# One transfer for the mask, the third tile's side loads in wider transfers on GpSimd's queue, and eight transfer places counted by the list scheduler

## The chip, the cores and the metric

The kernel runs on one core of a Trainium2 chip. The metric is the device time of one execution in microseconds (us). Several executions are timed, and one more is recorded by the hardware profiler; its times say where the work lies. The engines are TensorE (PE; its weight loads are PEld), VectorE (DVE), ScalarE (ACT), GpSimd (POOL) and SyncE (SP), which only issues transfers. SP and ACT issue transfers here; the transfers themselves run on 16 DMA engines.

## The reference

Attention over 4 batches, 8 heads, 576 positions of 64 numbers. The first four heads see a band of 32 positions, the other four see every 32nd position up to their own. The result, 2304 tokens of 512 numbers, goes through two MLPs of 512 to 2048 to 512.

```python
scores = scale * np.matmul(q, k.transpose(0, 1, 3, 2))
mask_local = (rel >= 0) & (rel < stride)
mask_strided = (rel >= 0) & (pos[None, :] % stride == pos[:, None] % stride)
scores = np.where(masks, scores, -1e9)
attn = softmax(scores)
x = np.matmul(attn, v)                    # -> (2304, 512)
r = np.maximum(x @ w_in, 0.0)             # first MLP
x = (s * (r * r) + b) @ w_out
h = x @ w_in2                             # second MLP
g = np.where(h >= 1, h, np.where(h <= -1, 0.0, (h + 1) ** 2 / 4))
out = g @ w_out2
```

## The kernel before

**Attention tiles.** The attention is cut into 21 tiles, sorted by their first token: 12 "strided" ones, three for each batch (d = 0, 1, 2), and 9 "local" ones of 256 tokens. Tiles 0, 1 and 2 are the strided ones of batch 0, tiles 3, 4 and 5 are local ones, tile 6 is the first strided one of batch 1, and so on. `attend` (from L427) writes down one tile: its loads (L446 to L459, all through the helper `load`), two TensorE matmuls that put the mask into two PSUM banks (L562), the scores on top of it (L567 strided, L582 local), the softmax on DVE and ACT (L589 to L600), four transposes (L609, called flips here), a copy of them to `pt`, and the values' matmuls (L623 strided, L633 local) into two banks named `side`. The `side` banks are a pair; from tile 6 on the scores use the same pair. They are drained by ACT, which rounds to fp32r (`xh`), and by DVE, which takes the remainder (`xl`, L665). `xh` and `xl` are the input of the first MLP.

**The third tile.** The third strided tile of a batch (d = 2) gathers what the first two leave over: its keys `k3` and queries `q3` are loaded in part (L490 to L498, columns 18 to 90) and for the rest copied out of the first two tiles' keys and queries (GpSimd or ACT, L312). Its value rows come from five places of the input in runs of 18 and 54 rows (L509 to L516). For batch 0 these loads go through ACT's queue, for the other batches through SP's.

**The mask.** `masks` (L406) loads the mask of the strided tiles into `mask_t`, 54 rows of 54 twice, at partitions 0 and 64, and a tile `fix_t` with the local mask, the identity and two scalars. GpSimd fills `mask_t` with a large negative number before. The casts `bias_t` and `idb_t` to bf16 follow; the first scores need both.

**The MLPs.** The first MLP works on six units of 384 tokens. Each of its products is made of three matmuls, high by high, low by high and high by low (L682 to L684). A hidden block is four such triples into one bank `h`. Its weights are loaded as 64-bit numbers (`raw`, 512 KB, three buffers) and decoded: a step on ACT (L328), two on DVE (L330, L332), a rounded copy on ACT (`w0h`, `w1h`) and a remainder on DVE (`w0l`, `w1l`, L351). A `raw` buffer is free again when L332 has read it. The second MLP multiplies by a scheme with seven products for eight; its weights are prepared during the first one (L357 to L398), written to memory as `dw` and read back later.

**What sets the order.** The program writes down operations with their engines, planned durations and dependences. `Issue.order` then works out due times backwards from the end, subtracts each operation's `sooner`, adds a normal draw of size JITTER (0.3, SEED 3, one number for each operation in turn), and places the operations one at a time: the one that can start first, and among equals the one that is due first. The order of starts becomes the order of instructions on every engine and queue. `attend_upto` (L1000) sets `sooner` for all operations of a tile to AHEAD * max(at - 5, 0), which is 0 for the first tiles, and so overwrites what `masks` had set. A transfer is planned with its queue's time and a latency; how many are under way at once isn't planned. The first loads of SP and ACT go out at once, and later ones wait in their queue for a place.

## Time and profile before

| what | us |
|---|---|
| timed executions | 847.67, 849.72, 850.36 |
| median | 849.72 |
| profiled execution | 847.82 |
| its span | 846.0 |
| TensorE busy in the span | 824.3 (97%) |
| VectorE busy | 599.4 (71%) |
| ScalarE busy | 517.4 (61%) |
| GpSimd busy | 22.8 (3%) |

All rows below come from the profiled execution, whose time is its span and 1.8 us around it. A stretch a:b is the time from a to b us after the span's start. Idle time in brackets behind an instruction is the time that its engine stood before it, with what ended the wait. The clock granted to TensorE is given as a share of its upper level.

### The profile page before, as it was taken

How to read it: one execution, taken by the hardware profiler on the slowest of the kernel's cores; microseconds unless marked ns; L12 is line 12 of the kernel's file. 1: busy time of each engine (PE TensorE's matmuls, PEld its weight loads, DVE VectorE, ACT ScalarE, POOL GpSimd, SP SyncE). 2: the span in 40 equal slices, each digit the busy share in tenths (PEclk: the TensorE clock that was granted, in tenths of full speed). 3: DMA queues.
4: the chain of work that ended last, by engine and by line, in shares of the span. 5: the costliest groups of instructions: out<-in, count | busy, mean ns of one | idle time of the engine just before them, and what ended most of it. 6: DMA issues, size and time to landing. Idle time of an engine off the chain costs nothing.

```text
span 846.0 us, 17391 instructions
## 1 busy us (share of the span) xinstructions
PE 824.3 (97%) x6336; PEld 800.7 (95%) x6336; DVE 599.4 (71%) x1250; ACT 517.4 (61%) x1054; POOL 22.8 (3%) x62
## 2 busy tenths in 40 slices
PE   6789999999999999999999999999999999999998
PEld 3579998989999899999999999999999999999998
DVE  5788647475598785767678356897666998465966
ACT  3577645554577674556567467875477854577653
POOL 1110000010000000000001000000000000000000
PEclk9599999999999999999999999999999999999999
DMA  8858271363389994768785558888988788878883
GB/s 260 259 177 276 99 240 64 91 183 108 122 289 329 277 310 132 223 222 255 257 303 196 154 185 253 252 255 271 293 267 256 252 254 286 289 252 252 251 271 103
DMA packets 115930, 191.77 MB, mean 227 GB/s; under 512 B 13830, under 2 KB 57990, under 8 KB 115846
## 3 DMA queue, kind: packets, MB, share of 16 engines
q1 hardware_dynamic: 114818, 190.23, 70.7%
q8 instruction: 51, 0.84, 0.4%
q10 hardware_dynamic: 1028, 0.43, 0.2%
q14 instruction: 33, 0.27, 0.1%
HBM read 150.25 MB, written 40.37 MB: 225 GB/s over the span
## 4 chain that ended last, share of the span: by engine, by line
PE 84%; DMA 8%; DVE 4%; ACT 2%; issue 1%; SPq 1%; ACTq 0%; DVEq 0%
PE h L682 7%; PE acc L682 6%; PE acc L684 6%; PE acc L683 6%; PE h L683 6%; PE h L684 6%; PE acc L934 6%; PE acc L932 6%; PE acc L933 6%; PE side L934 5%; PE side L933 5%; PE side L932 5%; DMA raw<-in_w_ins 4%; PE h L934 3%; PE h L932 3%; PE h L933 3%
## 5 line engine op out<-in xcount | busy, mean ns | idle before, releaser
L704 ACT ACTIVATE t<-h 128x384 f32<-128x384 f32 x96 | 46.5, 485 | 62.6 <-PE h L684 62.2
L682 PE MATMUL acc<-gh,w1hx 128*128 128x384 f32 x192 | 65.2, 340 | 0.0
L682 PE MATMUL h<-xh,w0hx 128*128 128x384 f32 x192 | 65.1, 339 | 0.0
L683 PE MATMUL acc<-gl,w1hx 128*128 128x384 f32 x192 | 64.9, 338 | 0.2
L683 PE MATMUL h<-xl,w0hx 128*128 128x384 f32 x192 | 64.5, 336 | 0.0
L684 PE MATMUL acc<-gh,w1lx 128*128 128x384 f32 x192 | 64.5, 336 | 0.0
L684 PE MATMUL h<-xh,w0lx 128*128 128x384 f32 x192 | 64.2, 334 | 0.0
L310 ACT ACTIVATE gh<-t 128x384 fp32r<-128x384 f32 x96 | 50.0, 521 | 21.9 <-DVE t L717 21.3
L721 DVE TENSOR_TENSOR gl<-t,gh 128x384 fp32r<-128x384 f32 x92 | 51.0, 555 | 16.1 <-ACT gh L310 15.8
L717 DVE TENSOR_SCALAR t<-t,fix_t 128x384 f32<-128x384 f32 x77 | 36.7, 477 | 35.8 <-ACT t L708 35.5
L682 PE MATMUL acc<-gh,w1h 128*128 128x384 f32 x168 | 57.2, 340 | 0.0
L684 PE MATMUL acc<-gh,w1l 128*128 128x384 f32 x168 | 56.9, 339 | 0.0
L683 PE MATMUL acc<-gl,w1h 128*128 128x384 f32 x168 | 56.8, 338 | 0.0
L682 PE MATMUL h<-xh,w0h 128*128 128x384 f32 x144 | 50.8, 353 | 0.2 <-ACT t L704 0.2
L683 PE MATMUL h<-xl,w0h 128*128 128x384 f32 x144 | 49.4, 343 | 0.0
L684 PE MATMUL h<-xh,w0l 128*128 128x384 f32 x144 | 49.3, 342 | 0.0
L708 ACT ACTIVATE t<-t 128x384 f32<-128x384 f32 x79 | 41.4, 524 | 2.1
L683 PEld LDWEIGHTS acc<-gl,w1hx 128*128 128x128 f32 x192 | 36.0, 188 | 1.1 <-DVE gl L721 1.0
L682 PEld LDWEIGHTS acc<-gh,w1hx 128*128 128x128 f32 x192 | 36.0, 188 | 0.4
L682 PEld LDWEIGHTS h<-xh,w0hx 128*128 128x128 f32 x192 | 36.0, 188 | 0.3
L683 PEld LDWEIGHTS h<-xl,w0hx 128*128 128x128 f32 x192 | 36.1, 188 | 0.0
L684 PEld LDWEIGHTS h<-xh,w0lx 128*128 128x128 f32 x192 | 36.1, 188 | 0.0
(513 smaller groups left out, 2514.3 us busy)
## 6 DMA issues: line engine op xcount, KB each, us to landing
w0h<-dw SPq DMA_DIRECT2D x84, 256.0 KB
w0l<-dw SPq DMA_DIRECT2D x84, 256.0 KB
w0hx<-dw SPq DMA_DIRECT2D x84, 256.0 KB
w0lx<-dw SPq DMA_DIRECT2D x84, 256.0 KB
raw<-in_w_ins SPq DMA_DIRECT2D x32, 512.0 KB
raw<-in_w_outs SPq DMA_DIRECT2D x32, 512.0 KB
dw<-pt SPq DMA_DIRECT2D x48, 256.0 KB
dw<-po SPq DMA_DIRECT2D x48, 256.0 KB
```

The source lines that it names most:

```text
L310: e.activation(out=out, in_=in_, func=AF.Copy)
L682: e.matmul(out=acc, lhsT=wh, rhs=ah, start=first, stop=False)
L683: e.matmul(out=acc, lhsT=wh, rhs=al, start=False, stop=False)
L684: e.matmul(out=acc, lhsT=wl, rhs=ah, start=False, stop=last)
L704: op(lambda e: e.activation(out=c(t), in_=c(p), func=AF.Relu), [act(n)], [p], [t])
L708: e.activation(out=c(t), in_=c(t), func=AF.Square)
L717: e.tensor_scalar(out=c(t), in0=c(t), scalar1=sb_t[:, 0:1], scalar2=sb_t[:, 1:2], op0=MUL, op1=ADD)
L721: op(lambda e: e.tensor_tensor(out=c(gl), in0=c(t), in1=c(gh).bitcast(F32), op=SUB), [pool(n)] + [dve2(n)], [t, gh], [gl])
L932: e.matmul(out=dst, lhsT=wh, rhs=ah, start=opens and first, stop=False, skip_group_check=not opens)
L933: e.matmul(out=dst, lhsT=wh, rhs=al, start=False, stop=False, skip_group_check=not opens)
L934: e.matmul(out=dst, lhsT=wl, rhs=ah, start=False, stop=last, skip_group_check=not opens)
```

## The change

1. **Mask.** `fix_t` is loaded first, and the mask in one transfer of 128 rows: its source runs twice over 64 rows of the input (step 0, then 64 rows). The rows 54 to 63 of each half come from the input too.
2. **Third tile's keys and values.** The keys are loaded by head pair, two transfers of 128 partitions, whose source is two blocks of 64 rows, in place of two of 64 partitions. The values are loaded in three transfers (36, 54 and 54 rows) in place of six (18, 18, 54, 18, 18, 18), written as one operation in place of three.
3. **Queue.** For batch 0 these six transfers are issued by GpSimd, planned at 1.0 us each, and no longer by ACT. For the other batches they stay on SP.
4. **Places.** The scheduler keeps a list of eight places (`LANES`). A transfer that is not GpSimd's starts in the plan only when places are free, and holds them until its planned end.
5. **`sooner`.** `attend_upto` adds to what stands there, so what `masks` sets now counts.

Lines after L72 stand one to six lines lower than before; L447, L324, L312 and L665 of before are L453, L330, L318 and L671 after.

```diff
@@ -69,6 +69,7 @@
 DMA_RATE = 390.0e3
 DMA_LATENCY = 2.0
 DMA_ISSUE = 0.45
+LANES = 8
 
 
 class Buf:
@@ -86,7 +87,7 @@
 
 
 class Op:
-    __slots__ = ("fn", "engs", "deps", "succ", "allocs", "bufs", "due", "wait", "ready", "start", "eng", "n", "behind", "sooner", "idle")
+    __slots__ = ("fn", "engs", "deps", "succ", "allocs", "bufs", "due", "wait", "ready", "start", "eng", "n", "behind", "sooner", "idle", "dmas")
 
 
 class Issue:
@@ -98,8 +99,9 @@
     def __init__(self):
         self.ops, self.apart = [], []
 
-    def op(self, fn, engs, reads=(), writes=(), part=(), after=(), allocs=(), line=None):
+    def op(self, fn, engs, reads=(), writes=(), part=(), after=(), allocs=(), line=None, dmas=0):
         o = Op()
+        o.dmas = dmas or any(x[0] == "sp" for x in engs)
         o.fn, o.engs, o.n, o.succ, o.due = fn, engs, len(self.ops), [], None
         deps = set(after)
         o.behind, o.sooner = (), 0.0
@@ -158,7 +160,7 @@
         rng = np.random.default_rng(SEED)
         for o in self.ops:
             o.due += JITTER * rng.standard_normal() - o.sooner
-        free = {"port": 0.0}
+        free, lanes = {"port": 0.0}, [0.0] * LANES
         for o in self.ops:
             o.wait, o.ready = len(o.deps), 0.0
             for x in o.engs:
@@ -187,6 +189,8 @@
                     continue
                 for e, d, _, *port in o.engs:
                     at = max(free[e], o.ready, t, free["port"] if port else 0.0)
+                    if o.dmas and e != "pool":
+                        at = max(at, lanes[o.dmas - 1] - DMA_ISSUE * (o.dmas - 1))
                     key = (at + (d - min(x[1] for x in o.engs)), o.due, o.n, d, at)
                     if best is None or key < best[0]:
                         best = (key, o, e, d)
@@ -200,6 +204,8 @@
             if port:
                 free["port"] = at + d
             end = at + d + lag
+            if o.dmas and e != "pool":
+                lanes = sorted(lanes[o.dmas:] + [end] * o.dmas)
             for b in o.allocs:
                 b.ring.taken.append(b)
             for b in o.bufs:
@@ -404,9 +410,9 @@
         return b * S if kind == "s" else t * 256
 
     def masks():
-        op(lambda e: e.dma_start(out=fix_t, in_=fixed[:, 128 + KT:FW]), [("act", 0.5, DMA_LATENCY)], writes=[fix_buf]).sooner = 50.0
-        op(lambda e: [e.dma_start(out=mask_t[g * 64:g * 64 + 54, 0:54], in_=fixed[0:54, 0:54]) for g in range(2)],
-           [("act", 1.0, DMA_LATENCY)], part=[mask_buf[0]]).sooner = 49.0
+        op(lambda e: e.dma_start(out=fix_t, in_=fixed[:, 128 + KT:FW]), [("act", 0.5, DMA_LATENCY)], writes=[fix_buf], dmas=1).sooner = 80.0
+        op(lambda e: e.dma_start(out=mask_t[:, 0:54], in_=bass.AP(fixed.tensor, fixed.offset, [[0, 2], [FW, 64], [1, 54]])),
+           [("act", 0.5, DMA_LATENCY)], part=[mask_buf[0]], dmas=1).sooner = 49.0
         op(lambda e: copy(e, bias_t[:, 0], mask_t), [("dve", 0.15, 0.1)], [mask_buf[0]], [bias_buf[0]]).sooner = 50.0
         op(lambda e: copy(e, idb_t, id_t), [("dve", 0.2, 0.1)], [fix_buf], [idb_buf]).sooner = 50.0
 
@@ -442,9 +448,9 @@
             return buf(wp if tag[0] == "w" else sp, tag, [128, 512], F32, BUFS.get(tag, MS // 2))
 
         def load(y, parts, size, queue="sp", line=a_line):
-            ways = [dma(size, len(parts)) if queue == "sp" else ("act", DMA_ISSUE * len(parts), DMA_LATENCY + 2 * size / DMA_RATE)]
+            ways = [dma(size, len(parts)) if queue == "sp" else (queue, 1.0 * len(parts), DMA_LATENCY + 2 * size / DMA_RATE)]
             first = bool(w_loads) and not held and line is a_line
-            o = op(lambda e, i=i: [e.dma_start(out=f(), in_=x) for f, x in parts], ways, part=[y], line=line,
+            o = op(lambda e, i=i: [e.dma_start(out=f(), in_=x) for f, x in parts], ways, part=[y], line=line, dmas=len(parts),
                    after=[w_loads[k] for k in HOLD] if first else ())
             if first:
                 held.append(o)
@@ -456,7 +462,8 @@
             return o
 
         half = lambda par: slice(par * D, (par + 1) * D)
-        side = ("act", b_line) if b == 0 else ()
+        side = ("pool", b_line) if b == 0 else ()
+        view = lambda x, at, *dims: bass.AP(x.tensor, x.offset + at, [list(n) for n in dims])
         W = RT * NJ
         QC, VC = 4 * 128, 4 * 128 + 2 * W
         if strided and d < 2:
@@ -491,9 +498,9 @@
                 rest[b] = [buf(sp, f"{n}3", [128, 2, 144], F32) for n in "kq"]
                 k3, q3 = rest[b]
                 src = strd[b, 4]
-                rest[b] += [load(k3, [(lambda par=par: k3.tile[half(par), :, 18:90],
-                                       src[half(par), 0:512].rearrange("p (h a n) -> p h a n", h=2, a=2)[:, :, par, 0:72])
-                                      for par in range(2)], 128 * 144 * 4, *side),
+                rest[b] += [load(k3, [(lambda h=h: k3.tile[:, h, 18:90],
+                                       view(src, 256 * h, (64 * SW + 128, 2), (SW, 64), (1, 72))) for h in range(2)],
+                                 128 * 144 * 4, *side),
                             load(q3, [(lambda: q3.tile[:, :, 18:90], src[:, QC:VC].rearrange("p (h n) -> p h n", h=2)[:, :, 0:72])],
                                  128 * 144 * 4, *side)]
             k3, q3, k_load, q_load = rest[b]
@@ -509,11 +516,10 @@
             ins, vals = [kb_, qb_], [vb_]
             v4 = lambda: vb_.tile.rearrange("p (g n) -> p g n", g=2)
             src = strd[b, 4]
-            parts = [(lambda: v4()[0:18, 0], strd[b, 3][108:126, VC:SW]), (lambda: v4()[18:36, 0], src[0:18, VC:SW]),
-                     (lambda: v4()[0:54, 1], src[18:72, VC:SW])]
-            parts += [(lambda t=t: v4()[64 + 18 * t:82 + 18 * t, 0], strd[b, t][108:126, VC:SW]) for t in range(3)]
-            for j in range(3):
-                load(vb_, parts[2 * j:2 * j + 2], 48 * 1024, *side)
+            parts = [(lambda: v4()[0:36, 0], view(strd[b, 3], 108 * SW + VC, (20 * SW, 2), (SW, 18), (1, 4 * D))),
+                     (lambda: v4()[0:54, 1], src[18:72, VC:SW]),
+                     (lambda: v4()[64:118, 0], view(strd[b, 0], 108 * SW + VC, (128 * SW, 3), (SW, 18), (1, 4 * D)))]
+            load(vb_, parts, 160 * 1024, *side)
             groups2 = [(j, g, n, (lambda par, hp, c=c, n=n: kb_.tile[half(par), hp, c:c + n]),
                         (lambda par, hp, c=c, n=n: qb_.tile[half(par), hp, c:c + n]), at_)
                        for j, g, n, c, at_ in ((0, 0, 36, 0, 0), (1, 0, 54, 90, 0), (0, 1, 54, 36, 36))]
@@ -1004,7 +1010,7 @@
             attend(at, first_token(at) < U0[1])
             at += 1
             for o in plan.ops[begin:]:
-                o.sooner = AHEAD * max(at - 5, 0)
+                o.sooner += AHEAD * max(at - 5, 0)
 
     pend = []
     todo = [(0, i) for i in range(KP)] + [(1, i) for i in range(KP)]
```

**What moves at the start.** ACT's queue from its first instruction on, before (`k_3` and `q_4` are the third tile's keys and queries, `w1hx` its values, `xh_2` holds tile 0's keys and queries, `sm` the scores before the exponential):

```order
L408 DMA mask_t<-in_fixed 54x54 x2
L407 DMA fix_t<-in_fixed 128x226
L447 DMA k_3_145<-in_strd 64x2x72 x2
L447 DMA q_4_151<-in_strd 128x2x72
L447 DMA w1hx_153<-in_strd 18x256 x2
L310 ACTIVATE bias_t<-fix_t 32x64 x4
L447 DMA w1hx_153<-in_strd 54x256
L447 DMA w1hx_153<-in_strd 18x256
L310 ACTIVATE k_3_145<-xh_2_131 64x2x18 x2
L447 DMA w1hx_153<-in_strd 18x256 x2
L595 ACTIVATE sm_166<-sm_166 128x512
```

The same of after:

```order
L413 DMA fix_t<-in_fixed 128x226
L414 DMA mask_t<-in_fixed 128x1x54
L316 ACTIVATE bias_t<-fix_t 32x64 x4
L316 ACTIVATE k_3_132<-xh_2_130 64x2x18 x4
L316 ACTIVATE q_4_147<-xh_2_130 128x2x18 x2
L601 ACTIVATE sm_166<-sm_166 128x512
```

Two transfers are left, and four copies that GpSimd had (two of `k_3`, two of `q_4`) stand behind the casts. GpSimd's queue after, from its last memset on; `xl_15` holds tile 1's keys and queries:

```order
L1063 MEMSET bias_t 32x32 x4
L453 DMA k_3_132<-in_strd 128x1x72 x2
L453 DMA q_4_147<-in_strd 128x2x72
L453 DMA w1hx_157<-in_strd 36x1x256
L453 DMA w1hx_157<-in_strd 54x256
L453 DMA w1hx_157<-in_strd 54x1x256
L318 COPY q_4_147<-xl_15_162 128x2x18
L318 COPY k_3_132<-xl_15_162 64x2x18 x2
```

Six transfers stand ahead of the copies from `xl_15`.

**What moves on VectorE ahead of the first hidden block.** Before (`side_650` and `side_651` are the banks of tile 4's values, `dt_686` the decode of the third weight):

```order
L330 TENSOR_SCALAR dt_686<-dt_686 128x512
L665 TENSOR_TENSOR xl_136<-side_651,xh_135 128x2x2x32
L665 TENSOR_TENSOR xl_134<-side_651,xh_133 128x2x2x32
L332 SCALAR_TENSOR_TENSOR dt_686<-raw_573,dt_686 128x512
L665 TENSOR_TENSOR xl_136<-side_650,xh_135 128x2x2x32
L665 TENSOR_TENSOR xl_134<-side_650,xh_133 128x2x2x32
L351 TENSOR_TENSOR w0l_563<-dt_618,w0h_562 128x512
```

After (there the banks are `side_648` and `side_649`, and the third weight is `dt_637`):

```order
L336 TENSOR_SCALAR dt_637<-dt_637 128x512
L338 SCALAR_TENSOR_TENSOR dt_629<-raw_556,dt_629 128x512
L338 SCALAR_TENSOR_TENSOR dt_637<-raw_570,dt_637 128x512
L671 TENSOR_TENSOR xl_138<-side_648,xh_137 128x2x2x32
L671 TENSOR_TENSOR xl_136<-side_648,xh_135 128x2x2x32
L671 TENSOR_TENSOR xl_138<-side_649,xh_137 128x2x2x32
L671 TENSOR_TENSOR xl_136<-side_649,xh_135 128x2x2x32
```

The last step of that decode, a SCALAR_TENSOR_TENSOR, stood between the drains of the two banks; now both drains follow behind it. On TensorE the scores of tile 6 and the first hidden block now stand ahead of the values of tile 5, which came first before.

**What moves on SP behind the loads of tile 7.** Before (`xl_140` is tile 7's keys and queries, `qx_775` its values, `qv_831` the values of tile 8, `raw` weights):

```order
L447 DMA xl_140_747<-in_strd 128x2x764
L447 DMA qx_775<-in_strd 54x2x256 x2
L324 DMA raw_805<-in_w_ins 128x512
L447 DMA qv_831<-in_strd 18x256 x2
L447 DMA qv_831<-in_strd 54x256
L447 DMA qv_831<-in_strd 18x256 x3
L324 DMA raw_886<-in_w_outs 128x512
L324 DMA raw_907<-in_w_outs 128x512
```

After:

```order
L453 DMA xl_140_703<-in_strd 128x2x764
L330 DMA raw_749<-in_w_ins 128x512
L330 DMA raw_773<-in_w_outs 128x512
L330 DMA raw_821<-in_w_outs 128x512
L453 DMA qx_841<-in_strd 54x2x256 x2
L453 DMA qv_884<-in_strd 36x1x256
L453 DMA qv_884<-in_strd 54x256
L453 DMA qv_884<-in_strd 54x1x256
```

Three weights stand ahead of tile 7's values now, where one stood behind them. From there to 230 us the order on the engines differs in many places by a few rows; the decodes come one or two hidden blocks sooner. From about 235 us on TensorE's order is the same in both.

## Rows read from the trace of the kernel before

**Rows 1.** The page, parts 1 and 3: busy us of each engine, then the transfer queues.

```profile
PE 824.3 (97%) x6336; PEld 800.7 (95%) x6336; DVE 599.4 (71%) x1250; ACT 517.4 (61%) x1054; POOL 22.8 (3%) x62
...
q1 hardware_dynamic: 114818, 190.23, 70.7%
...
q10 hardware_dynamic: 1028, 0.43, 0.2%
```

**Rows 2.** Busy time by stretches: stretch, its length, engines (instructions), PE clock, DMA share, GB/s.

```profile
8.00:12.00 4.00, 4.00 (x96) 2.69 (x84) 2.33 (x6) 1.88 (x7) 0.68 (x4) 0.57 0.78 229
12.00:30.00 18.00, 12.73 (x354) 8.93 (x352) 15.42 (x47) 7.15 (x20) 3.20 (x7) 0.87 1.03 305
...
39.00:46.00 7.00, 6.63 (x82) 5.84 (x84) 4.23 (x10) 3.46 (x9) 0.87 (x3) 0.52 0.68 218
46.00:54.00 8.00, 8.00 (x104) 7.24 (x105) 6.78 (x16) 6.14 (x14) 1.29 (x2) 1.00 0.57 192
54.00:66.00 12.00, 8.58 (x143) 6.70 (x142) 11.71 (x29) 9.71 (x26) 1.82 (x2) 1.00 0.50 165
66.00:70.00 4.00, 4.00 (x16) 3.99 (x15) 3.86 (x10) 2.31 (x5) 0.00 (x0) 0.57 1.02 380
...
290.00:320.00 30.00, 27.57 (x152) 25.99 (x151) 24.92 (x51) 22.93 (x48) 0.00 (x0) 1.00 0.86 274
```

**Rows 3.** Timeline of 0:12, all engines: start, us, engine, line, operation, idle before and releaser.

```profile
1.19 0.91 ACTq L408 DMA_DIRECT2D mask_t<-in_fixed  x2
...
2.13 0.37 ACTq L407 DMA_DIRECT2D fix_t<-in_fixed  x1
...
2.54 3.04 ACTq L447 DMA_DIRECT2D k<-in_strd  x2
...
6.33 0.20 DVE L312 CAST bias_t<-mask_t 128x64 bf16<-128x64 f32 x1 [5.20 <-DMA mask_t<-in_fixed]
...
7.44 0.39 PE L562 MATMUL acc<-bias_t,idb_t 128*128 128x256 bf16 x2 [2.18 <-DVE idb_t L312]
...
9.25 0.21 POOL L312 COPY q<-xl 128x36 f32<-128x36 f32 x1 [3.39 <-DMA xl<-in_strd]
...
10.43 0.63 ACT L595 ACTIVATE sm<-sm 128x512 f32<-128x512 f32 x1 [0.41 <-issue]
...
11.28 0.87 PE L567 MATMUL acc<-k,q 64*36 64x36 f32 x24
```

**Rows 4.** Timeline of 12:30, TensorE.

```profile
20.88 0.46 PE L582 MATMUL acc<-xl 64*32 64x64 f32 x32 [1.40 <-DMA xl<-in_loc]
...
28.35 0.30 PE L633 MATMUL side<-pt,w1lx 64*64 64x32 f32 x4 [1.35 <-DMA qv<-in_loc]
```

**Rows 5.** Timeline of 33:42, TensorE and VectorE.

```profile
38.48 0.68 DVE L332 SCALAR_TENSOR_TENSOR dt<-raw,dt 128x512 int32<-128x512 int32 x1
...
38.82 0.42 PE L633 MATMUL side<-pt,qx 64*64 64x32 f32 x4 [1.29 <-DVE xl L665]
39.08 0.48 DVE L665 TENSOR_TENSOR xl<-side,xh 128x128 fp32r<-128x128 f32 x2
...
39.48 1.28 DVE L351 TENSOR_TENSOR w0l<-dt,w0h 128x512 fp32r<-128x512 f32 x2
...
39.62 0.96 PE L633 MATMUL side<-pt,qx 64*64 64x32 f32 x26 [0.37 <-DVE xl L665]
```

**Rows 6.** Timeline of 30:46, SP's queue.

```profile
35.32 0.47 SPq L447 DMA_DIRECT2D xl<-in_strd  x1
40.72 1.14 SPq L447 DMA_DIRECT2D qx<-in_strd  x2
41.97 0.36 SPq L324 DMA_DIRECT2D raw<-in_w_ins  x1
```

**Rows 7.** Timeline of 54:66, VectorE and TensorE.

```profile
56.08 0.75 DVE L593 TENSOR_TENSOR sx<-side,mx 128x256 f32<-128x256 f32 x2
...
56.75 0.80 PE L623 MATMUL side<-pt,qv 54*64 54x54 f32 x32 [1.27 <-ACT gh L310]
```

## The prediction

> **What bounds the kernel now.** I read the busy shares first, then the stretches, then inside the bad stretches the timeline with its waits. TensorE works for 824.3 of 846.0 us [rows 1], so 21.7 us of idle TensorE is all that any change of order or of transfers can win, beside stretches at the lower clock. Stretch less busy time gives where they lie [rows 2]: 5.27 us in 12:30, 0.37 in 39:46, 3.42 in 54:66, and late in the kernel 2.43 in 290:320. The clock ran near its lower level in 8:12, 39:46 and 66:70 (granted 0.57, 0.52, 0.57; 1.00 is the level of 2.4 GHz), the last two of them behind stretches in which TensorE stood and waited.
>
> Three things hold TensorE there. At the start it is the transfers: the DMA engines are full from 2 us on but sag to 0.78 in 8:12 [rows 2], and the scores of local tiles wait 1.40 us at 20.88 for a load, the values of tile 3 another 1.35 at 28.35 [rows 4]. From 38 us it is VectorE's place in the chain of the first hidden block [rows 5]. In 54:66 it is VectorE outright: 11.71 of 12 us busy [rows 2], while TensorE waits for banks it has to drain [rows 7]. (The profile names ACT's gh as the releaser at 56.75; the values' matmul there needs no gh, it needs the banks that VectorE was reading at 56.08.)
>
> **The change, part by part.** The sum is made on the profiled execution, 847.82 us = span 846.0 + 1.82. The median of the runs, 849.72, lies 1.90 above it, and I carry the difference over to the median.
>
> *Start-up.* Before, ACT issues the mask (0.91), the fixed tile (0.37), the third tile's keys (3.04, most of it waiting) and the rest [rows 3]; the exponential of the first tile starts at 10.43 after 0.41 of idle that its input doesn't explain: ACT still issues. After, ACT issues two transfers and GpSimd the other six. The fixed tile's issue moves from 2.13 to about 1.19, 0.94 sooner; TensorE has stood 2.18 us when the cast of its identity lets it start at 7.44, and the mask's cast was done at 6.53, so 0.9 is open here if the mask stays in time. The DMA engines' sag in 8:12 is worth 4 x (1 - 0.78) = 0.88 us of transfer; with six issues gone from the shared places, SP's loads wait less, and that is what TensorE waits for at 20.88 and 28.35. These are one chain, not a sum: I take -0.9, from 0 to -1.4 (0.9 + the exponential's 0.41). ACT takes over four small copies from GpSimd, about 0.2 each like GpSimd's at 9.25; the 7 us up to the exponential cover them, and without that cover they would cost 0.8.
>
> *GpSimd's queue.* The trace shows no transfer issued by GpSimd. The nearest rows are ACT's issues: 0.37 for one transfer, up to 3.04 for two with waiting [rows 3]; six of them take 2.2 to 9.1 us. Behind them on GpSimd stand the copies that fetch tile 1's part of the third tile's keys, at 9.25 before. From about 1.7, behind its first memsets, the issues end at 3.9 to 10.8, so 0 to +1.6; I take 0, since an issue that waits for no place is what the lower row shows.
>
> *Mask and keys in wider pieces.* Mask: one issue fewer, 0.46, counted above. How a transfer spreads is seen in the queue's count: q10 carries 1028 packets [rows 1], of which 892 are rows of data (108 mask, 128 fixed tile, 256 keys, 256 queries, 144 values). The other 136 come out exactly as 9 per transfer of 54 or 18 rows and 16 per transfer of 64 or 128 rows, one per DMA engine that took part. So a row count is dealt to 16 engines or to its largest divisor below. What a source in two blocks of 64 (mask, keys) does, no row shows: 16 engines by its 128 rows, or 2 by its outer count. I take 16 for the sum and give the other its own rival. The Trainium skill, "DMA: Bandwidth & Descriptors", section "Why a DMA increments its semaphore by 16 and not by 1", says that the slowest dimension of both patterns decides, which would make it 2 here; with that rule the start-up term would be lost and not -0.9. Its rule for single dimensions agrees with the 9 and 16 of this count.
>
> *Order of the first hidden block.* The draw of numbers shifts, since eight operations fall away, so lines move where no transfer did. Before, VectorE does the last step of the third weight's decode, 0.68, between the drains of the two banks, for which TensorE waits 1.29 at 38.82 and 0.37 at 39.62 [rows 5]; after, it stands ahead of both. The second drain then ends some 0.6 sooner, so the 0.37 goes and the 1.29 for the first stays. What comes behind is the scores of tile 6 in place of the values of tile 5, work that is done either way. -0.4; 0 if the decode's data are late, -1.66 if both waits go.
>
> *Weights ahead of the values on SP.* SP stands 4.9 us behind xl until the buffer of qx is free at 40.72; the first weight behind it goes out at 41.97 [rows 6]. After, three weights stand ahead of qx. The first then waits only for its own buffer, free before the third weight's step ends at 39.16 [rows 5]: at least 2.8 us sooner. One weight costs VectorE 0.68 for that step and 1.28 / 2 = 0.64 for the remainder, 1.32 us with its short first step left out [rows 5]. In 39:54 VectorE has 15 - 4.23 - 6.78 = 3.99 us free, in 54:66 0.29 [rows 2]. Each weight decoded in the first frees 1.32 in the second, where TensorE stood 3.42. The pairs of banks there are also drained behind more matmuls than before. I take -1.4, one weight's worth. Bounds: all of the 3.42 and the slow clock behind it, 66:70 at 0.57 costs 4 x (1 - 0.57) = 1.72, so -5.1; on the other side +1.4, one weight decoded in the wrong place. qx itself goes out later by what the three weights wait, and the loads of the third tile's values behind it with it; both are first used in 54:66 or after, some 15 us on, and cost nothing.
>
> *Later batches.* Three issues fewer each on SP, hidden by loads that run ahead: 0. The order of loads also changes between 231 and 318 us, where weights come from memory; TensorE's order there stays. 0, from -2.43 (all idle of 290:320) to +3.8 (two loads of 512 KB put ahead at that stretch's 274 GB/s, 1.9 each) [rows 2].
>
> Sum: -0.9 - 0.4 - 1.4 = -2.7. That gives 845.1 on the profiled execution and **847.0** on the median.
>
> **Rivals.** (A) The forecast, -2.7: 847.0, with its own range 845.0 to 849.0.
>
> (B) *The count of places does not do what it says.* It is a number in the planner; the first fourteen loads of SP stand in the same order as before. If the sag in 8:12 has another cause, and VectorE, 15.42 of 18 us busy in 12:30 [rows 2], sets the pace anyhow, only the -0.4 is left: 849.3. Against it: ACT's issue of keys, 3.04 for two, shows a queue that waits.
>
> (C) *Slower: few engines take the mask and the keys.* By the row count above, 2 engines get 64 packets each. A packet of SP's queue takes 0.707 x 16 x 846 / 114818 = 83 ns, one of q10 0.002 x 16 x 846 / 1028 = 26 ns [rows 1]. Alone, 64 take 1.7 us; taking turns with SP's, 64 x 109 ns = 7.0. The mask took 6.33 - 2.10 = 4.2 us from its issue's end [rows 3], with 12 packets to an engine; it would land between 7.6 and 12.9 and the first scores start up to 5.6 late. The keys' two transfers, behind each other on the same engines, land as late as 20.6, where the third tile's scores stood at 11.28, 9.3 late. The waits at 20.88 and 28.35 absorb 1.40 + 1.35 = 2.75, and the later terms' -1.8 stays: 9.3 - 2.75 - 1.8 = +4.75, 854.5. It is slower from a lateness of 4.55 on. For it: the page's rule. Against it: packets can run in bursts, which is then B's result, and GpSimd's queue may spread otherwise.
>
> (D) *The whole VectorE gap closes*: -0.9 - 0.4 - 5.1 = -6.4, 843.3.
>
> **How the numbers follow.** 0.3%, 2.55 us, is about what a measurement of this kernel can tell. A 0.46 (of which 0.26 under 847.2, 0.20 within), B 0.24 (0.20 within, 0.02 to either side), C 0.20 (0.18 slower, 0.02 within), D 0.10. Faster 0.26 + 0.02 + 0.10 = 0.38; same 0.20 + 0.20 + 0.02 = 0.42; slower 0.02 + 0.18 = 0.20. The range takes in D's value and C up to a lateness of 7.8 us: 843.0 to 853.0. A alone is 845.0 to 849.0.
>
> **What would show it.** Start-up right: the first scores before 7.0, the exponential right behind its input, the wait at 20.88 under 0.6, DMA over 0.9 in 8:12. C: mask's cast after 8 us, or the third tile's scores waiting for keys. First block right: its first matmul before 40.5, with nothing of a decode between the drains. Weights right: VectorE busier in 39:54, TensorE over 10 of 12 us in 54:66, and the clock at its upper level in 66:70. Wrong would be: the same TensorE idle before 70 us, or a new wait for a weight in 290:320.

## The result and the profile after

The changed kernel is slower. Its median is 855.32 us against 849.73 us of the kernel before, both over five executions; the ratio is 1.0067, 95% interval 1.0047 to 1.0088. Measured again beside the experiments (g1_changed below), it is 855.81 against 847.75, ratio 1.0086 (1.0053 to 1.0118). The forecast was 847.0 with a range of 843.0 to 853.0; the time lies outside it, on the other side of the time before.

The profiled execution took 857.9 us, with a span of 855.4 against 846.0 before. It is the longest of the five, and the one of before is near its shortest: the profiles lie 10.1 us apart, the medians 5.6. The page, engines and transfer queues:

```profile
PE 824.1 (96%) x6332; PEld 800.8 (94%) x6335; DVE 601.3 (70%) x1258; ACT 514.5 (60%) x1048; POOL 27.7 (3%) x66
...
q1 hardware_dynamic: 114614, 190.23, 70.4%
...
q0 software_dynamic: 464, 0.30, 0.2%
...
q10 hardware_dynamic: 274, 0.14, 0.1%
```

TensorE works 824.1 us, as before [rows 1]. What came in this profile is idle time, 855.4 - 824.1 = 31.3 us against 21.7. The stretches, in the same columns as [rows 2]:

```profile
2.00:8.00 6.00, 3.17 (x9) 1.08 (x8) 0.23 (x1) 2.40 (x12) 4.02 (x6) 1.00 0.99 267
8.00:12.00 4.00, 0.00 (x0) 0.00 (x0) 0.00 (x0) 0.00 (x0) 0.00 (x0) 0.50 1.06 259
12.00:30.00 18.00, 12.52 (x336) 8.79 (x339) 13.00 (x37) 5.93 (x17) 1.55 (x7) 0.83 0.94 264
...
46.00:54.00 8.00, 8.00 (x125) 7.33 (x124) 5.55 (x14) 4.87 (x11) 1.05 (x6) 0.82 0.72 250
54.00:66.00 12.00, 10.50 (x147) 8.83 (x136) 11.78 (x28) 9.86 (x24) 3.60 (x5) 1.00 0.62 191
66.00:70.00 4.00, 3.71 (x83) 3.02 (x81) 4.00 (x11) 2.90 (x6) 0.52 (x1) 1.00 0.76 240
70.00:230.00 160.00, 153.91 (x1804) 145.02 (x1806) 95.91 (x238) 80.71 (x172) 7.84 (x22) 0.97 0.42 132
...
290.00:320.00 30.00, 27.70 (x155) 26.43 (x154) 27.11 (x55) 23.47 (x48) 0.00 (x0) 1.00 0.95 306
```

Two places carry the new idle time. In 8:12 no engine but the DMA engines does anything: 4.00 us of idle, where TensorE was busy throughout before. And in 70:230, 160 - 153.91 = 6.09 us are idle. Before, that stretch had 0.04, and 66:80 nothing:

```profile
66.00:80.00 14.00, 14.00 (x74) 13.99 (x73) 10.73 (x24) 10.59 (x21) 0.00 (x0) 0.88 0.86 289
70.00:230.00 160.00, 159.96 (x1941) 151.19 (x1940) 99.28 (x240) 87.09 (x183) 7.01 (x22) 1.00 0.44 137
```

On the other side 54:66 gained what the forecast had hoped for, 1.50 us of idle against 3.42, and 290:320 stayed.

The first place, in the timeline:

```profile
1.60 1.85 POOL L453 DMA_DIRECT2D k<-in_strd  x2
1.63 1.12 ACTq L414 DMA_DIRECT2D mask_t<-in_fixed  x1
...
2.44 0.47 SPq L453 DMA_DIRECT2D xl<-in_strd  x1
2.96 1.22 SPq L453 DMA_DIRECT2D w0lx<-in_strd  x2
3.42 0.77 POOL L453 DMA_DIRECT2D q<-in_strd  x1
4.17 1.85 POOL L453 DMA_DIRECT2D w1hx<-in_strd  x3
5.01 0.23 DVE L318 CAST idb_t<-fix_t 128x128 bf16<-128x128 f32 x1 [3.87 <-DMA fix_t<-in_fixed]
...
13.09 0.21 POOL L318 COPY q<-xl 128x36 f32<-128x36 f32 x1 [7.07 <-DMA xl<-in_strd]
...
14.68 0.20 DVE L318 CAST bias_t<-mask_t 128x64 bf16<-128x64 f32 x1 [9.44 <-DMA mask_t<-in_fixed]
14.93 0.59 PE L568 MATMUL acc<-bias_t,idb_t 128*128 128x256 bf16 x2 [9.76 <-DVE bias_t L318]
```

The fixed tile came 2.15 us sooner (its cast at 5.01, before at 7.16), as forecast, but the mask lands only at 14.6 us, where its cast stood at 6.33 [rows 3], and the first scores start at 14.93 for 7.44. Tile 1's keys, which SP asked for 1.5 us sooner (2.44 for 3.91), arrive 3.8 us later: GpSimd's copy from them starts at 13.09 for 9.25 [rows 3].

The second place, right behind 66:70 (the values at 72.52 are tile 8's, 36 rows; the triple at 76.75 is the second half of the hidden block that needs them):

```profile
70.39 0.76 DVE L595 TENSOR_REDUCE mx<-side 128x4 f32<-128x256 f32 x2
...
71.06 0.69 DVE L357 TENSOR_TENSOR w0lx<-dt,w0hx 128x512 fp32r<-128x512 f32 x1
71.66 0.43 DVE L336 TENSOR_SCALAR dt<-dt 128x512 int32<-128x512 int32 x1
71.99 0.43 DVE L599 TENSOR_TENSOR sm<-side,mx 128x256 f32<-128x256 f32 x1
72.33 0.69 DVE L338 SCALAR_TENSOR_TENSOR dt<-raw,dt 128x512 int32<-128x512 int32 x1
72.52 0.31 PE L629 MATMUL side<-pt,qv 36*64 36x36 f32 x4 [2.81 <-issue]
72.92 0.43 DVE L599 TENSOR_TENSOR sm<-side,mx 128x256 f32<-128x256 f32 x1
...
73.45 0.91 PE L629 MATMUL side<-pt,qv 54*64 54x54 f32 x20 [0.62 <-issue]
...
74.62 0.66 ACT L334 ACTIVATE dt<-raw 128x512 f32<-128x512 f32 x1 [3.21 <-DMA raw<-in_w_ins]
...
76.22 0.68 ACT L316 ACTIVATE xh<-side 128x36 fp32r<-128x36 f32 x4
...
76.75 0.69 PE L688 MATMUL h<-xh,w0h 128*128 128x384 f32 x1 [2.39 <-ACT xh L316]
...
77.89 0.69 PE L689 MATMUL h<-xl,w0h 128*128 128x384 f32 x1 [0.45 <-DVE xl L671]
```

The four bracketed waits of TensorE add up to 2.81 + 0.62 + 2.39 + 0.45 = 6.27 us, all of the idle time of 66:80. The profile gives "issue" for the first two; the matmuls there write the two `side` banks, and their starts follow the two sm steps at 71.99 and 72.92, with which VectorE finishes reading tile 9's scores from those banks. Decode steps for other weights stand between. Then ACT, in order, waits 3.21 us for a weight to arrive before it comes to the drain of tile 8's values.

### The profile page after: what moved, and what is told of

The parts are those of the page before. It is cut to its first block, busy times and chain, and to the rows that moved or that the text cites. A ratio compares the mean times of both kernels' runs of the same rounds, so it can differ in the third digit from the quotient of the medians.

```text
span 855.4 us, 17361 instructions
## 1 busy us (share of the span) xinstructions
PE 824.1 (96%) x6332; PEld 800.8 (94%) x6335; DVE 601.3 (70%) x1258; ACT 514.5 (60%) x1048; POOL 27.7 (3%) x66
## 4 chain that ended last, share of the span: by engine, by line
PE 82%; DMA 9%; DVE 5%; ACT 2%; issue 2%; SPq 0%; POOL 0%; DVEq 0%; ACTq 0%; POOLq 0%
PE h L688 6%; PE acc L688 6%; PE h L689 6%; PE h L690 6%; PE acc L689 6%; PE acc L690 6%; PE acc L938 6%; PE acc L939 6%; PE acc L940 6%; DMA raw<-in_w_ins 5%; PE side L938 5%; PE side L940 5%; PE side L939 5%; PE h L939 3%; PE h L940 3%; PE h L938 3%
## 5 line engine op out<-in xcount | busy, mean ns | idle before, releaser
L723 DVE TENSOR_SCALAR t<-t,fix_t 128x384 f32<-128x384 f32 x71 | 33.8, 476 | 38.9 <-ACT t L714 38.7
L714 ACT ACTIVATE t<-t 128x384 f32<-128x384 f32 x71 | 37.1, 523 | 1.8
```

What stands on the lines that cost most here:

```text
L714: e.activation(out=c(t), in_=c(t), func=AF.Square)
L723: e.tensor_scalar(out=c(t), in0=c(t), scalar1=sb_t[:, 0:1], scalar2=sb_t[:, 1:2], op0=MUL, op1=ADD)
```

## The experiments

All ratios are to the kernel before, measured beside it on the same chip. The kernels named a and b, c and d, e and f, and g ran on four different chips, so ratios are compared and not times. "us" is (ratio - 1) x 848.

| kernel | order of work | mask | pieces of keys and values | batch 0's queue | median (before) | ratio, 95% interval | us |
|---|---|---|---|---|---|---|---|
| b1_mask_one | before | one | old | ACT | 847.80 (847.93) | 0.9992, 0.9971 to 1.0013 | -0.7 |
| a1_mask_two | changed | two | wide | GpSimd | 856.46 (847.93) | 1.0112, 1.0089 to 1.0134 | +9.5 |
| a2_keys_old | changed | two | old | GpSimd | 855.04 (847.93) | 1.0086, 1.0063 to 1.0109 | +7.3 |
| a3_acts_queue | changed | two | old | ACT | 853.89 (847.93) | 1.0069, 1.0044 to 1.0094 | +5.9 |
| c1_draws | changed, draw of before | one | wide | GpSimd | 851.61 (847.86) | 1.0045, 1.0021 to 1.0069 | +3.8 |
| d5_draws_mask_two | changed, draw of before | two | wide | GpSimd | 852.53 (847.86) | 1.0053, 1.0031 to 1.0075 | +4.5 |
| d2_before_shifted | before, draw of changed | two | old | ACT | 854.68 (847.86) | 1.0080, 1.0055 to 1.0104 | +6.8 |
| d4_tile8_sooner | changed, tile 8 ahead | one | wide | GpSimd | 850.07 (847.86) | 1.0028, 1.0013 to 1.0044 | +2.4 |
| e1_old_forms | changed, draw of before | two | old | GpSimd | 849.48 (848.30) | 1.0017, 0.9999 to 1.0035 | +1.4 |
| e3_new_forms_act | changed, draw of before | two | wide | ACT | 849.10 (848.30) | 1.0019, 1.0000 to 1.0039 | +1.6 |
| e2_old_all | changed, draw of before | two | old | ACT | 846.87 (848.30) | 0.9988, 0.9970 to 1.0005 | -1.0 |
| f1_tile8_old | changed, tile 8 ahead | two | old | ACT | 847.71 (848.30) | 0.9994, 0.9976 to 1.0011 | -0.5 |
| g1_changed | changed | one | wide | GpSimd | 855.81 (847.75) | 1.0086, 1.0053 to 1.0118 | +7.3 |
| g2_scores9_later | changed, tile 9's scores later | one | wide | GpSimd | 852.50 (847.75) | 1.0057, 1.0040 to 1.0073 | +4.8 |
| g3_scores9_old | changed, tile 9's scores later | two | old | ACT | 852.10 (847.75) | 1.0031, 1.0014 to 1.0049 | +2.6 |

In the kernels that share an entry under "order of work", every engine's instructions stand in the same order, transfers on ACT and GpSimd apart, so they differ in the transfers alone.

### The mask by itself

The first theory was rival C of the prediction: the mask lands late, all else follows. Two kernels test it from both sides. On the changed kernel the mask goes back to two transfers, and on the kernel before it becomes one:

```diff
-        op(lambda e: e.dma_start(out=mask_t[:, 0:54], in_=bass.AP(fixed.tensor, fixed.offset, [[0, 2], [FW, 64], [1, 54]])),
+        op(lambda e: [e.dma_start(out=mask_t[g * 64:g * 64 + 54, 0:54], in_=fixed[0:54, 0:54]) for g in range(2)],
```

> The changed kernel, only the mask loaded in two transfers of 54 rows as before; every engine's order is that of the changed kernel. Theory M (the mask's single transfer, which landed at 14.6 us, is the whole loss): the mask lands by 6.5, the first scores start before 7.5, the time is 847 to 849.5, and TensorE's 6 us of idle in 70:80 are gone with the late start. Theory O (the new order costs by itself, the late start is mostly absorbed): the first scores are as early, but TensorE still stands 4 us or more in 70:80 and the time is 852 or more.

> The kernel before, only the mask loaded in one transfer, its source twice 64 rows; every engine's order is that of the kernel before. Theory M: the first scores start at 12 us or later and the time is 853 to 856. Theory O: the first scores are as late, but the waits for loads at 20.9 and 28.4 and idle VectorE take most of it, 850 to 852.

Theory M fell on both sides. With two transfers the mask is there at 7.74 and the first scores start at 7.99, and the time is 9.5 us over the kernel before, no better than the changed kernel (7.3, with intervals that overlap). The timeline of a1_mask_two, TensorE:

```profile
7.99 0.38 PE L568 MATMUL acc<-bias_t,idb_t 128*128 128x256 bf16 x2 [2.35 <-DVE bias_t L318]
...
12.77 1.01 PE L573 MATMUL acc<-xl 64*54 64x54 f32 x32 [3.13 <-DMA xl<-in_strd]
```

The scores of tile 1 wait for their keys until 12.77, and the first hidden block starts at 43.77, where it starts at 43.42 with the mask in one (g1_changed): the early mask only moved the wait from one load to the next. In the kernel before, one transfer lands at 8.0 and not at 14.6:

```profile
1.19 1.17 ACTq L408 DMA_DIRECT2D mask_t<-in_fixed  x1
...
8.02 0.20 DVE L312 CAST bias_t<-mask_t 128x64 bf16<-128x64 f32 x1 [6.89 <-DMA mask_t<-in_fixed]
...
8.72 0.39 PE L562 MATMUL acc<-bias_t,idb_t 128*128 128x256 bf16 x2 [3.10 <-DVE idb_t L312]
```

There the late mask costs nothing that can be measured, though the first hidden block starts 2.6 us later (44.10 for 41.47).

### The pieces and the queue, in the changed order

a2_keys_old puts the old pieces back as well (still one operation in the plan, still issued by GpSimd); a3_acts_queue also issues them from ACT, behind the mask:

```diff
-            o = op(lambda e, i=i: [e.dma_start(out=f(), in_=x) for f, x in parts], ways, part=[y], line=line, dmas=len(parts),
+            o = op(lambda e, i=i: [(nc.scalar if side and line is b_line else e).dma_start(out=f(), in_=x) for f, x in parts], ways, part=[y], line=line, dmas=count,
```

> The changed kernel with the mask in two transfers, and the third tiles' keys and values in the old pieces (64 and 18 or 54 rows), still through GpSimd's queue for batch 0; the order is that of the changed kernel. Theory M: within 1 us of the kernel with only the mask put back. Theory K (keys on few engines hold the third tile's scores): 2 to 4 us faster than that one, with the third tile's scores earlier.

> The changed kernel's order of work with all transfers of before: mask in two, old pieces, batch 0's side loads issued by ACT. Theory M: 847 to 850; if GpSimd's queue helped as forecast, about 0.9 above the kernel with old pieces on GpSimd's queue. Theory O: 852 or more, with TensorE standing 4 us or more in 70:80.

With every transfer as before, the changed order alone is 5.9 us slower. Theory O held: TensorE stands 6.6 us in 66:80 in a3_acts_queue, 6.9 in a2_keys_old and 6.8 in a1_mask_two, whatever the start is like. Theory K is not decided: with the old pieces the third tile's scores start 1.0 us sooner (13.46 for 14.46) and the time is 2.2 us lower, at the low end of what K gave, but the two intervals overlap. And GpSimd's queue did not help: with ACT's the time is 1.4 us lower (within the intervals), where 0.9 higher was expected.

### The draw

What sets that order? In the plan, the old value loads are three operations for each batch and the new ones one. The scheduler draws one random number for each operation in turn, so from tile 2 on every operation gets another's number. c1_draws keeps the whole change and lets two numbers fall behind each of these loads, so that all others get theirs back; d2_before_shifted is the kernel before, with the two loads that fall away drawing none:

```diff
 c1_draws
             o.due += JITTER * rng.standard_normal() - o.sooner
+            rng.standard_normal(o.more)      # 2 for a third tile's value load, else 0
 d2_before_shifted
-            o.due += JITTER * rng.standard_normal() - o.sooner
+            o.due += (0.0 if o.none else JITTER * rng.standard_normal()) - o.sooner
```

> The changed kernel in full, but with the scheduler drawing two more numbers behind each third tile's value load, so that every later operation gets the number that it has in the kernel before; TensorE's order is then nearly that of before. Theory D (the loss is the shifted draw and the order it makes, through the stall of TensorE in 66:80): 847 to 850, less than 1.5 us idle in 66:80. Theory R (the loss lies in the change's own parts: transfers, queue, places): 852 or more.

> The kernel before with nothing changed but the draw: the second and third value load of a third tile take no number, so that the others get those of the changed kernel; TensorE's order is then that of the changed kernel. Theory D: 852 to 856, with 5 us or more of TensorE idle in 66:80. Theory R: 847 to 850.

d2_before_shifted is the cleanest run of the study: no transfer, no queue, no cost differs from the kernel before, and it is 6.8 us slower. Its stretches (idle in 66:80: 14 - 7.18 = 6.82):

```profile
54.00:66.00 12.00, 10.52 (x172) 8.75 (x168) 12.00 (x30) 9.53 (x23) 3.23 (x4) 1.00 0.51 167
66.00:80.00 14.00, 7.18 (x46) 6.30 (x43) 11.26 (x27) 7.99 (x18) 0.94 (x1) 0.63 0.79 277
```

The second line has a granted clock of 0.63 over 14 us, where the kernel before has 0.88 there, with 0.57 in 66:70 [rows 2]. So beside the idle time the matmuls behind the stop run nearer the lower level. The same step from e2_old_all to a3_acts_queue (both with all transfers as before and the places counted) is 5.9 + 1.0 = 6.9 us. In c1_draws TensorE stands only 0.97 us in 66:80, as theory D said, but the time, expected between 847 and 850, came out at 851.6, between the two theories: the draw is not the whole loss. 3.8 us stay in the change's own parts. The draw's 6.8 us are one draw against one other; what a third would give was not tried.

### What is left with the draw of before

> The changed kernel with the draw of before and the mask in two transfers. If the mask's late landing costs where the order is that of before: 1 to 4 us faster than the same with the mask in one. If VectorE and the waits for loads absorb it, as in the kernel before with one transfer: within 1 us of it.

> The changed kernel with the draw of before, the mask in two transfers, and the third tiles' keys and values in the old pieces, issued by GpSimd for batch 0. Theory F (the wide forms, dealt to few DMA engines, hold SP's early loads back): tile 1's keys arrive before 11.8, and the time is 848 to 850, against 852.5 with the wide forms. Theory G (GpSimd's queue does it): they arrive after 12.5 and the time stays at 851 or more.

> The changed kernel with the draw of before and the mask in two transfers; the wide forms stay, but batch 0's are issued by ACT. Theory F: 851 to 853.5, tile 1's keys after 12. Theory G: 847.5 to 849.5, tile 1's keys before 11.

> The changed kernel with the draw of before and all transfers as before (mask in two, old pieces, ACT's queue); what is left of the change is the fixed tile ahead of the mask, the counted places and the kept sooner. Both theories: 847 to 849, the same as before. Below 846.5 these three would be worth something by themselves; above 849.5 a part of the loss lies in them.

The four have one order of work. The mask's form makes no difference here either (d5_draws_mask_two, 4.5 against 3.8 us of c1_draws; the intervals cover each other). From e2_old_all, GpSimd's queue adds 2.4 us (e1_old_forms), the wide pieces 2.6 (e3_new_forms_act), and both together 5.5 (d5_draws_mask_two). Each kernel's interval reaches about 1.5 us to either side, so the first two are above zero, but no difference between them is shown. By the times that they gave, F held in e1_old_forms and G in e3_new_forms_act: neither was right alone. GpSimd's copy from tile 1's keys shows when that load has landed, in e2_old_all, e1_old_forms, e3_new_forms_act and d5_draws_mask_two in turn:

```profile
9.15 0.21 POOL L319 COPY q<-xl 128x36 f32<-128x36 f32 x1 [7.50 <-DMA xl<-in_strd]
```

```profile
11.47 0.21 POOL L319 COPY q<-xl 128x36 f32<-128x36 f32 x1 [2.76 <-DMA xl<-in_strd]
```

```profile
10.21 0.21 POOL L319 COPY q<-xl 128x36 f32<-128x36 f32 x1 [8.56 <-DMA xl<-in_strd]
```

```profile
13.50 0.21 POOL L319 COPY q<-xl 128x36 f32<-128x36 f32 x1 [7.48 <-DMA xl<-in_strd]
```

With GpSimd's queue SP's own loads go out sooner, as if places were free: in e1_old_forms the loads behind tile 1's keys are issued at 3.80, 5.90, 6.51 and 6.91, in e2_old_all at 5.46, 10.09, 10.49 and 10.96. They then run beside tile 1's keys, which TensorE needs first. That they delay it is read from the order of these times, not tried by itself; GpSimd's own transfers, which are under way at the same time, are the other candidate. Nor is it shown that the late keys are what the time is lost by: in e3_new_forms_act they come only 1.1 us later than in e2_old_all, and TensorE's idle time is no longer there (846.5 - 823.3 = 23.2 us, against 844.9 - 821.3 = 23.6); what is longer is its busy time.

How the wide pieces are dealt is shown by the count of packets. The queue page of e3_new_forms_act, where all the pieces in question are on ACT's queue:

```profile
q10 hardware_dynamic: 960, 0.43, 0.2%
```

892 rows of data leave 68: 16 for the fixed tile, 18 for the mask in two, 16 for the queries, 9 for the 54 rows in one block, and 9 for the other four, which comes out as 2 + 2 for the two blocks of 64 (keys), 2 for the two blocks of 18 and 3 for the three. The changed kernel's 274 above are 128 + 128 rows, 16 for the fixed tile and 2 for the mask. So by these counts a source in two blocks, of 64 or of 18 rows, runs on 2 DMA engines. The Trainium skill's rule that the prediction weighed ("DMA: Bandwidth & Descriptors", "Why a DMA increments its semaphore by 16 and not by 1") is what these counts show.

GpSimd's queue, which has batch 0's keys and values in the changed kernel, counts otherwise (464 packets on the page above for 656 runs of data, a run being one contiguous piece), so its count does not give the engines. The sizes of its packets, in the trace, do for the keys. With the old pieces (a2_keys_old) they are 32 packets of 2304 bytes, 8 runs of 288 each: 16 shares to a transfer, a share being what goes to one DMA engine. With the wide ones a share is cut into packets of at most 15 runs, and four packets of 1152 bytes, 4 runs, close four shares of 4 x 15 + 4 = 64 runs: 2 shares to a transfer there too.

### The stall in 66:80

In the changed order tile 9's scores stand ahead of tile 8's transposes and values, and the score banks and the value banks are the same pair. Four kernels move that place. d4_tile8_sooner and f1_tile8_old pull tile 8 ahead; g2_scores9_later and g3_scores9_old only let tile 9's scores wait for tile 8's values in the plan:

```diff
 d4_tile8_sooner, f1_tile8_old
-                o.sooner += AHEAD * max(at - 5, 0)
+                o.sooner += AHEAD * max(at - 5, 0) + 6.0 * (at == 9)
 g2_scores9_later, g3_scores9_old (pvs holds the values' operations)
-        first = op(scores, ..., sc, allocs=[sm, mx, dn])
+        first = op(scores, ..., sc, allocs=[sm, mx, dn], after=[pvs[8]] if i == 9 else ())
```

> The changed kernel with its draw, and 6 us added to sooner for the operations of tile 8, so that tile 9's scores no longer stand ahead of tile 8's values in the banks. If the stall in 66:80 is that place: its 6 us of idle fall under 2 and the time to 848 to 851. If the draw costs in many small places: 853 or more, with the idle elsewhere.

> The changed kernel with its own draw, tile 8 pulled 6 us ahead in the plan, and all transfers as before (mask in two, old pieces, ACT's queue). With tile 8 alone pulled ahead the time was 850.07; taking back what the transfers cost at the start gives 845.5 to 848.5, so it may come out under the kernel before. If the start is hidden behind the later stretches: 849 to 850.5.

> The changed kernel itself, beside the others of this call. 853 to 857; with the mask in two it was 856.5 in an earlier call, so the mask's single transfer should be worth less than 2 us either way.

> The changed kernel, only tile 9's scores made to wait for tile 8's values in the plan; up to there TensorE's order is that of the changed kernel. Theory B (the stall in 66:80 is tile 9's scores holding the banks that tile 8's values need): the wait ahead of tile 8's values falls from 2.8 + 0.6 to under 0.5, and the time falls by 2 to 4 us against the changed kernel. Theory W (the stall is ACT waiting for a weight ahead of the drain of tile 8's values): the first wait goes, the second, about 2.4 ahead of the hidden block, grows, and the time falls by less than 1.5.

> The same with all transfers of before (mask in two, old pieces, ACT's queue). By the parts, 2.5 to 5 us under the one with the new transfers; 848 to 851 by theory B, 850 to 853 by theory W.

TensorE in g2_scores9_later:

```profile
70.28 0.68 PE L631 MATMUL side<-pt,qv 36*64 36x36 f32 x24 [1.03 <-ACT pt L316]
72.45 0.69 PE L690 MATMUL h<-xh,w0h 128*128 128x384 f32 x1 [1.49 <-ACT xh L316]
73.88 0.69 PE L691 MATMUL h<-xl,w0h 128*128 128x384 f32 x1 [0.74 <-DVE xl L673]
```

ACT's drain of tile 8's values in the same kernel:

```profile
71.93 0.68 ACT L316 ACTIVATE xh<-side 128x36 fp32r<-128x36 f32 x4
```

The wait for the banks, 2.81 + 0.62 in g1_changed, is gone; 1.03 for the copy of the transposes is left, which it had hidden (under 0.5 was expected). The two waits behind fall from 2.57 + 0.46 to 1.49 + 0.74, and the idle time of 66:80 from 6.46 to 3.26. The median falls by 3.3 us, by the ratios 2.5. That is what theory B gave, for half of the stall or a little more, and not theory W, by which the second wait would have grown. The banks are not the whole of it, though: ACT's drain now stands ahead of the step that waits for a weight, which waits 3.53 us at 76.14 behind it, where in the changed kernel it stood before the drain. The other half is the rest of the chain (transposes, copy, drain, with decode steps in between), which stays as long as tile 8 comes this late. Pulling tile 8 itself ahead takes more back: d4_tile8_sooner stands 2.47 us in 66:80 (under 2 was expected) and is 4.9 us better than g1_changed, at 850.07 within the 848 to 851 given for it. With the transfers of before on top, f1_tile8_old is level with the kernel before, 6.4 us better than a3_acts_queue: nearly all of the 6.9 that the draw had cost. g3_scores9_old came out 2.2 us under g2_scores9_later by the ratios and 0.4 by the medians, less than the 2.5 to 5 expected; its median, 852.10, lies in the range of theory W and above that of B. So B rests on g2_scores9_later alone. No kernel here beats the one before by more than its interval.

## Why the prediction was wrong, point by point

- **What bounds the kernel.** Right as far as it went. Most of the idle time before 70 us was found; 30:39, where TensorE was busy for 5.76 of 9 us, is left out, though its 3.24 us are nearly as much as the 3.42 of 54:66. Missed above all: 66:80 had no idle time before, so no term asked what its order was good for.
- **Start-up, -0.9.** Wrong in sign. The steps were seen: the fixed tile's cast 2.15 us sooner, ACT free, DMA at 1.06 of its time in 8:12 (over 0.9 as forecast). The step that failed is "SP's loads wait less, and that is what TensorE waits for". The loads that gained are not those that TensorE waits for first; tile 1's keys came 3.8 us later. (The bound, 0.9 + 0.41, is 1.31 and not 1.4, which changes nothing.)
- **GpSimd's queue, 0 with a bound of +1.6.** Its issues took 1.85 + 0.77 + 1.85 = 4.47 us, within the 2.2 to 9.1 worked out. But the cost was not the copies behind them on GpSimd, which wait for tile 1's keys: it was +2.4 us with the draw of before (1.4 in the changed order), while tile 1's keys landed later, and the term had no place for that.
- **Mask and keys in wider pieces, 16 engines taken.** Wrong choice: 2 engines each, by the packets. The keys' and values' pieces cost 2.6 us. The mask's landing, at 14.6 us, lies beyond the 12.9 that rival C gave as its end, and it cost nothing on its own (b1_mask_one -0.7; c1_draws, with one transfer, is 0.7 under d5_draws_mask_two, with two).
- **Order of the first hidden block, -0.4, and weights ahead on SP, -1.4.** This is the step that decided it. Both looked at places where the new order could help. The first did not: with the transfers of before the first hidden block starts at 41.49 in d2_before_shifted, 41.47 before. The second did: 54:66 lost 1.9 us of idle, in d2_before_shifted too, and its signs came true (TensorE 10.50 of 12 us busy there, the clock at 1.00 in 66:70), a few us ahead of the stall. What failed is that the shifted draw was costed only where the kernel before had waited. The same shift put tile 9's scores ahead of tile 8's values at 68 us, and the order is worth +6.8 as a whole where -1.8 was given. The bound of +1.4 on the wrong side came from one decode in the wrong place; no bound was set for a chain moved as a whole.
- **Later batches, 0.** Right: 290:320 has 2.30 us of idle against 2.43.
- **Rivals.** C foresaw the mask's few engines and the direction, by a mechanism that turned out to cost little by itself; that its 854.5 lies near the measured time is luck. B's doubt about the places holds: e2_old_all, where the count of places, the fixed tile first and the kept `sooner` are all that is left, can't be told from the kernel before.

The parts by the runs: the draw +6.9 (e2_old_all to a3_acts_queue), the transfers +1.4 on top of it (a3_acts_queue to g1_changed), the rest of the change -1.0: 7.3 us, what g1_changed shows by construction. With the draw of before the same transfers cost 4.8 (e2_old_all to c1_draws). In the changed order a part of the late start may be lost in the stall anyhow; but g1_changed alone has an interval of 4.5 to 10.0 us, so that the two differ is not shown.

## What to carry to other kernels

Where a list scheduler adds random numbers drawn in sequence to the times that it sorts by, any change in the number of operations redraws all that follow, and that alone was worth 6.8 us of 848 here: before costing an edit, keep the old draw for the operations that stay, or cost the new order as a change by itself, also at the places that did not wait before. Look at what the merged pattern of a wider transfer starts with: two blocks of 64 rows ran on 2 DMA engines where 64 rows alone ran on 16, and the wide pieces cost 2.6 us. And a place freed early in a queue goes to whichever load stands next; here the load that TensorE needed first then came later, though that the one caused the other was only read from the times.

## What the runs showed of the hardware that was not expected

The same single transfer of the mask, 128 rows on 2 DMA engines, landed 6.8 us after its issue began in b1_mask_one (1.19 to its cast at 8.02) and 13.0 us after in the changed kernel (1.63 to 14.6). The two differ in the fixed tile, which went out ahead of the mask in the changed kernel, and in what else was under way; no run separates the two. And a start that was late by 7.5 us left TensorE's first hidden block only 3.1 us late (44.59 for 41.47): the waits for loads of before, 1.40 and 1.35 us at 20.88 and 28.35 [rows 4], are gone in between.
